# Two weight transfers for the first head of a fused attention and gated-MLP kernel, and a copy moved from GpSimd to ScalarE

## The chip, the cores and the metric

The kernel runs on one core of a Trainium2 chip. The metric is the device time of one execution in microseconds, as the median of three runs. Engines are named as in the profile: PE is TensorE (PEld its weight loads), DVE VectorE, ACT ScalarE, POOL GpSimd, SP SyncE, which issues most transfers.

## The reference

```python
x = A_x                                # [1, 2048, 640], bf16
xn = _layernorm(x)
q = (xn @ wq)                          # 32 heads of 192
scores = einsum("bhqd,bhkd->bhqk", q, k_cache) * (192 ** -0.5)   # 2048 keys
o = einsum("bhqk,bhkd->bhqd", softmax(scores), v_cache)
s = o.reshape(1, 2048, 32 * 192) @ wo  # back to 640
h = silu(xn @ w1) * (xn @ w3)          # 1536 hidden
g = silu(h @ w2)
return x + s * g
```

## The kernel before

The work goes head by head, in each head over four blocks of 512 queries (`qb`), in each block over eight pairs of key tiles (`p`). A projection fills two PSUM banks of 128 rows by 512 queries. A head has only 192 query columns, so the second bank's 64 free rows compute 64 columns of the MLP: even heads take a slice of `B_w1`, odd heads one of `B_w3`. The first bank (`t = 0`) is columns 0 to 127 of the head, the second (`t = 1`) has the MLP slice in rows 0 to 63 and columns 128 to 191 of the head in rows 64 to 127. After the projection the banks are cast to bf16 as `qA` (first bank) and `qF` (second); `qS` is `qA` with its two row halves swapped, `qD` the lower rows of `qF` moved up. The score matmuls contract over 64 rows each, so that two of them, one on the upper and one on the lower row half of the array, make a step; for that the keys lie as `KT` and, with halves exchanged, as `KM`.

The first head (h = 0) has routines of its own. Its weights come in pieces on SP's queue (`load_weights`, L99), issued between those of the keys. Its first block is projected at L380 with 128 contraction rows, in two halves of 256 queries. Its other blocks, and they alone besides a small part of the MLP, go through `by_halves` (L347): ten matmuls on the two row halves, then other work (`between`, mainly the values of an earlier step, L620), then ten more with the banks exchanged between the halves. The other heads are projected by `by_steps` (L362). From the third head on scores, values and projections are split into four 64x64 quarters (`quads`); the first two heads use 64x128.

The order of nearly all instructions is written out by hand (`pin` keeps them in program order on their engine). At the start, POOL builds `KM` from `KT` (L138, L135), shifts three columns of key maxima (`up`, `down`; L468, L471, L472), sets the column of ones in the values' tile (L141), and copies `qS` (L392) for the first block. DVE takes maxima of the keys (L411) and of the queries (L400), joins them (L477), and from them comes the bound `nbb` (L500, L502), without which ACT can't start the first exponential (L569). PE meanwhile runs `fill` matmuls (L224) that keep it busy, four of them in front of the first scores (L561). The order at the start is

```python
copy_high(L0); key_maxima(0, 1); up(m0); key_maxima(0, 2); copy_low(L0)
down(m0)
set_ones(L0)
key_maxima(0, 0)
project_chunk(0, 0, nc.scalar.copy)()
heads[0]["km"] = join_maxima(m0, sh)
```

where the call's result, called at once, takes the maxima of the queries. The functions that the change touches:

Of the kernel before, what the change touches and what calls it, by code (L numbers as in the profile page):

```python
# [12 lines left out]
BF16 = mybir.dt.bfloat16  # L13
# [3 lines left out]
P = 128  # L17
DH = 192
# [12 lines left out]
def _kernel_impl(ctx, tc, A_x, A_k_cache, A_v_cache, A_wq, A_wo, B_w1, B_w3, B_w2, out):  # L31
    nc = tc.nc
# [4 lines left out]
    DC = D // P  # L37
# [10 lines left out]
    PGW = P - DT  # L48
# [5 lines left out]
    ROWS = (slice(0, DT), slice(DT, P))  # L54
# [19 lines left out]
    xnT = const.tile([P, DC, SQ], BF16, name="xnT")  # L74

    pin = tc.keep_in_program_order
# [12 lines left out]
    def load_weights(h):  # L89
        wsel = B_w1 if h % 2 == 0 else B_w3  # L90
        m = h // 2
        parts = ((A_wq[:, h * DH:h * DH + P], 0, 0, P), (wsel[:, m * PGW:(m + 1) * PGW], 1, 0, PGW),
                 (A_wq[:, h * DH + P:(h + 1) * DH], 1, PGW, P))
        if h == 0:
            wq = lnx.tile([P, 2, DC, P], BF16, name="wq0")

            def piece(part):
                w, t, c0, c1 = part
                pin(nc.sync.dma_start(out=wq[:, t, :, c0:c1], in_=w.rearrange("(c p) d -> p c d", p=P)))  # L99
            return dict(wq=wq, pieces=[lambda part=part: piece(part) for part in parts])  # L100
        else:
            wq = wqp.tile([P, 2 * DC, P], BF16, tag="wq")
            for w, t, c0, c1 in parts:
                pin((nc.gpsimd if h <= 3 else nc.sync).dma_start(out=wq[ROWS[t], :, c0:c1], in_=w.rearrange("(s p) d -> p s d", p=DT)))
        return dict(wq=wq)
# [28 lines left out]
    def copy_low(L, keep=pin):  # L134
        keep(nc.gpsimd.tensor_copy(out=L["KM"][ROWS[0], :], in_=L["KT"][ROWS[1], 0, :]))  # L135
# [4 lines left out]
    def set_ones(L, keep=pin):  # L140
        keep(nc.gpsimd.memset(L["vt"][:, :, :, DH:DH + 1], 1.0))  # L141

    def move(out, in_):
        pin(nc.sync.dma_start(out=out, in_=in_))
# [28 lines left out]
    with ExitStack() as actx:  # L173
# [5 lines left out]
        lnx = lctx.enter_context(tc.tile_pool(name="lnx", bufs=1, side="right"))  # L179
# [7 lines left out]
        cols = lnx.tile([P, 32], BF16, name="cols")  # L187
        rows = lnx.tile([P, 32], BF16, name="rows")
        nc.vector.memset(cols[:, 0:1], 0.0)
        for k in range(5):  # L190
            w = 1 << k
# [146 lines left out]
        def by_halves(banks, w, qs, touch, between):  # L338
            def behind_of(op, dep):
                tc.add_manual_dep(op.ins, dep.ins.name, mybir.DependencyInfo(  # L340
                    mybir.DependencyClass.Sync, mybir.DependencyReason.DATA), reason="bank")

            for half in range(2):
                for c in range(DC):
                    for r in range(2):
                        t = r ^ half
                        mm = pin(nc.tensor.matmul(banks[t], lhsT=w(t, c)[ROWS[r], :], rhs=xnT[ROWS[r], c, qs],  # L347
                                                  start=(half == 0 and c == 0), stop=(half == 1 and c == DC - 1)))
                        if half == 1 and c == 0:
                            behind_of(mm, fence)  # L350
                if half == 0:
                    mark = fsb.tile([P, 1], F32, tag="mark", name="mark")
                    fence = pin(touch(out=mark[:], in_=eps_t[:]))
                    behind_of(fence, mm)
                    between()
# [9 lines left out]
        def project_chunk(h, qb, cast=nc.vector.tensor_copy, mid=(), quads=False, cast_low=None):  # L365
            hd = heads[h]
            wq = hd["L"]["wq"]
            qA, qF, qS, qD, st = hd["qA"], hd["qF"], hd["qS"], hd["qD"], hd["st"]
            qs = slice(qb * 512, (qb + 1) * 512)
            ps = ps_st.tile([P, 1024], F32, tag="st2", name="ps")  # L370
            halves = [ps[:, 0:512], ps[:, 512:1024]]
            if h == 0 and qb > 0:
                by_halves(halves, lambda t, c: wq[:, t, c, :], qs, nc.scalar.copy if qb == 1 else nc.vector.tensor_copy, steps((parts.pop(0)[1],), *mid))
            elif h == 0:
                acc["bp"] = ps_o.tile([P, 2, 512], F32, tag="ob0", name="bp")
                halves[1] = acc["bp"][:, 1, :]
                for u in (slice(0, 256), slice(256, 512)):
                    for t in range(2):
                        for c in range(DC):
                            pin(nc.tensor.matmul(halves[t][:, u], lhsT=wq[:, t, c, :], rhs=xnT[:, c, u],  # L380
                                                 start=(c == 0), stop=(c == DC - 1)))
            else:
                by_steps(halves, wq, qs, quads)
            for c, dst, src in ((cast_low or cast, qF, halves[1]), (cast, qA, halves[0]))[::1 if cast_low else -1]:
                pin(c(out=dst[:, qs], in_=src))  # L385
            if h > 1:
                move(qD[:, qs], qF[PGW:P, qs])
                for t in range(2):
                    move(qS[ROWS[t], qs], qA[ROWS[1 - t], qs])
                return None  # L390
            for t in range(2):
                pin(nc.gpsimd.tensor_copy(out=qS[ROWS[t], qs], in_=qA[ROWS[1 - t], qs]))  # L392

            first = h == 0 and qb == 0
            copy = nc.scalar.copy if first else nc.gpsimd.tensor_copy
            pin(copy(out=qD[:, qs], in_=qF[PGW:P, qs]))

            def maxima():
                for col, src, r0 in ((3, halves[0] if first else qA[:, qs], 0), (4, halves[1] if first else qF[:, qs], PGW)):
                    pin(nc.vector.tensor_reduce(out=st[r0:P, col, qb:qb + 1], in_=src[r0:P, :], axis=AX.X, op=ALU.max,  # L400
                                                apply_absolute_value=True))
            return maxima
# [6 lines left out]
        def key_maxima(h, j, k=0, n=1):  # L409
            c0, c1 = k * HALF // n, (k + 1) * HALF // n  # L410
            pin(nc.vector.tensor_reduce(out=heads[h]["st"][:, j, k:k + 1], in_=heads[h]["L"]["KT"][:, j, c0:c1], axis=AX.X,  # L411
                                        op=ALU.max, apply_absolute_value=True))
# [328 lines left out]
        parts = []  # L741
# [53 lines left out]
        up(m0)  # L795
        key_maxima(0, 2)
        copy_low(L0)
        down(m0)
        set_ones(L0)
        key_maxima(0, 0)  # L800
        project_chunk(0, 0, nc.scalar.copy)()
        heads[0]["km"] = join_maxima(m0, sh)
        loads[1] = load_weights(1)
        swap_rows(0)
# [27 lines left out]
        def steps(*fs):  # L832
            return lambda: [f(*a) for f, *a in fs]
# [77 lines left out]
        w1_sb = fw.tile([P, DC, FL - P], BF16, name="w1_sb")  # L911
        w3_sb = fw.tile([P, DC, FL - P], BF16, name="w3_sb")
# [18 lines left out]
        def ffn_hidden(qb, fl, ps, between=None):  # L931
            hT = get_hT(qb)
            qs = slice(qb * 512, (qb + 1) * 512)
            if between:
                by_halves((ps[:, 0:512], ps[:, 512:1024]), lambda t, c: (w1_sb, w3_sb)[t][:, c, (fl - 1) * P:fl * P], qs,
                          nc.vector.tensor_copy, between)
            else:
                for o, w_sb in ((0, w1_sb), (512, w3_sb)):
                    for c in range(DC):
                        pin(nc.tensor.matmul(ps[:, o:o + 512], lhsT=w_sb[:, c, (fl - 1) * P:fl * P], rhs=xnT[:, c, qs],  # L940
                                             start=(c == 0), stop=(c == DC - 1)))
            t = fsb.tile([P, 512], BF16, tag="t", name="t")
            pin(nc.scalar.activation(out=t[:], in_=ps[:, 0:512], func=ACT.Tanh, scale=0.5))
            u = fsb.tile([P, 512], BF16, tag="u", name="u")
            pin(nc.vector.tensor_copy(out=u[:], in_=ps[:, 512:1024]))
            a = fsb.tile([P, 512], BF16, tag="a", name="a")
            pin(nc.vector.scalar_tensor_tensor(out=a[:], in0=t[:], scalar=1.0, in1=ps[:, 0:512], op0=ALU.add, op1=ALU.mult))
            return lambda: pin(nc.vector.tensor_tensor(out=hT[:, FCP + fl - 1, :], in0=a[:], in1=u[:], op=ALU.mult))
# [249 lines left out]
    with ExitStack() as dctx:  # L1198
# [3 lines left out]
        with tc.issue_after(acc["store"].ins):  # L1202
            parts = [load_part(pools, 0, j) for j in range(3)]
# [30 lines left out]
        def st_bank():  # L1234
            return ps_st.tile([P, 1024], F32, tag="st2", name="ps_s")
# [4 lines left out]
        for qb in range(LB):  # L1240
            if qb == 0:
                banks = [st_bank(), st_bank(), ob_bank(0)]
            elif qb == 1:
                banks = [ob_bank(1), st_bank(), st_bank()]
            else:
                banks = [ob_bank(0), ob_bank(1), st_bank()]
# [162 lines left out]
```

## Time and profile before

| | |
|---|---|
| median of 3 runs | 1918.88 us (1918.73 to 1919.02) |
| profiled execution | 1919.53 us, span 1917.9 us |
| granted TensorE clock | 1.0 |
| PE busy | 1910.8 us |
| ACT, DVE, POOL busy | 1382.4, 1426.1, 99.7 us |

In a timeline each row has its start and its length in us, engine, line, operation, out<-in by the program's names, the tile of the array (rows*columns) for matmuls, operand shapes, the count that the row merges, and in brackets the engine's idle time before it with what ended it. Rows of one engine can overlap, since the end of a matmul is modelled and lies behind the start of the next.

### The profile page before, as it was taken

Reading aid. Unit: us, or ns where it says so; the run is one execution under the profiler, and the core shown is the slowest. Engines: PE = TensorE matmul, PEld = TensorE weight load, DVE = VectorE, ACT = ScalarE, POOL = GpSimd, SP = SyncE. Lnnn points to the kernel's source line nnn. Section 1 sums busy time; section 2 is a strip of 40 time slices with the busy share of each in tenths; the row PEclk is TensorE's granted clock in tenths of the full one; section 3 lists DMA queues with packets and bytes.
Section 4 is the critical chain, followed back from the end, with each engine's and each line's share of the span. In section 5 each row is a group of like instructions: output and inputs, shape, how many; then the busy total and the mean of one; then the engine's idle time right before and its main releaser. Section 6 shows DMA issues by size and latency. Waiting matters only on the chain.

```text
span 1917.9 us, 68799 instructions
## 1 busy us (share of the span) xinstructions
PE 1910.8 (100%) x30919; PEld 1112.4 (58%) x30919; DVE 1426.1 (74%) x2558; ACT 1382.4 (72%) x1521; POOL 99.7 (5%) x224
## 2 busy tenths in 40 slices
PE   9999999999999999999999999999999999999999
PEld 5665555555555555555555556666666666454456
DVE  8658888888888888888888888888888885521111
ACT  7778888888888888888888888888888887210000
POOL 3300000000000000000000000000000000000000
PEclk9999999999999999999999999999999999999999
DMA  7835655566655656566556565656565634937763
GB/s 169 151 74 101 134 111 123 114 121 115 127 119 113 129 108 128 107 128 117 130 106 132 101 132 100 138 96 141 104 125 112 131 60 125 273 82 150 165 151 76
DMA packets 649579, 235.86 MB, mean 123 GB/s; under 512 B 577072, under 2 KB 641168, under 8 KB 649280
## 3 DMA queue, kind: packets, MB, share of 16 engines
q1 hardware_dynamic: 640816, 210.98, 55.1%
q0 software_dynamic: 3776, 15.40, 2.8%
q10 hardware_dynamic: 4688, 5.05, 0.9%
q8 instruction: 242, 3.96, 0.9%
q14 instruction: 57, 0.47, 0.1%
HBM read 54.26 MB, written 31.98 MB: 45 GB/s over the span
## 4 chain that ended last, share of the span: by engine, by line
PE 99%; DMA 0%; POOL 0%; ACT 0%; issue 0%; SPq 0%; DVE 0%; POOLq 0%
PE st L561 34%; PE obank L640 31%; PE ps L362 14%; PE ps_s L1153 8%; PE obank L620 3%; PE ps_s L1109 3%; PE ps_f L1173 2%; PE ps_gu L940 1%; PE ps_f L1189 1%; PE ps L347 0%; DMA KT<-in_A_k_cache_dram 0%; PE ps_gu L347 0%; ACT xnT L290 0%; SPq L115 0%; PE pst L289 0%
## 5 line engine op out<-in xcount | busy, mean ns | idle before, releaser
L569 ACT ACTIVATE pT<-st,nb 128x1024 bf16<-128x1024 f32 x1016 | 1125.3, 1113 | 188.0 <-PE st L561 151.3
L640 PE MATMUL obank<-pT,vt 64*64 64x512 bf16 x11136 | 765.5, 376 | 0.0
L640 PEld LDWEIGHTS <-vt 64*64 64x64 bf16 x11136 | 360.7, 107 | 258.3
L561 PE MATMUL st<-qS,KM 64*64 64x512 bf16 (+1 forms) x1951 | 397.6, 376 | 0.5 <-POOL qS L392 0.5
L561 PE MATMUL st<-qD,KT 64*64 64x512 bf16 (+1 forms) x1951 | 397.6, 376 | 0.0
L561 PE MATMUL st<-qA,KT 64*64 64x512 bf16 (+1 forms) x1951 | 397.5, 376 | 0.0
L561 PE MATMUL st<-qA,KM 64*64 64x512 bf16 (+1 forms) x1951 | 391.4, 376 | 0.0
L561 PE MATMUL st<-qS,KT 64*64 64x512 bf16 (+1 forms) x1951 | 391.3, 376 | 0.1
L561 PE MATMUL st<-qF,KT 64*64 64x512 bf16 (+1 forms) x1951 | 391.3, 376 | 0.0
L561 PEld LDWEIGHTS <-KT 64*64 64x64 bf16 (+1 forms) x7808 | 249.4, 106 | 176.0 <-issue 0.6
L362 PE MATMUL ps<-xnT,wq 64*64 64x512 bf16 (+1 forms) x2390 | 289.5, 376 | 0.0
L362 PE MATMUL ps<-xnS,wq 64*64 64x512 bf16 (+1 forms) x2390 | 287.9, 376 | 0.0
L673 DVE TENSOR_TENSOR tree<-pT,pT 128x2048 bf16<-128x2048 bf16 x232 | 282.6, 1218 | 3.2 <-ACT pT L569 3.2
L665 DVE TENSOR_TENSOR ot<-oa,obank 128x512 bf16<-128x512 f32 x232 | 149.0, 683 | 108.6 <-ACT oa L664 108.1
L673 DVE TENSOR_TENSOR tree<-tree 128x2048 bf16<-128x2048 bf16 x232 | 221.2, 954 | 4.0
L362 PEld LDWEIGHTS <-wq 64*64 64x64 bf16 (+1 forms) x4780 | 151.4, 107 | 113.9
L561 PEld LDWEIGHTS <-KM 64*64 64x64 bf16 (+1 forms) x3904 | 132.4, 106 | 74.1 <-issue 1.4
L1153 PE MATMUL ps_s<-oT,wo_sb 128*128 128x512 bf16 x720 | 155.7, 379 | 0.0
L664 ACT COPY oa<-obank 128x512 f32<-128x512 f32 x232 | 123.6, 589 | 0.0
L1153 PEld LDWEIGHTS <-wo_sb 128*128 128x128 bf16 x720 | 70.4, 98 | 84.9 <-issue 0.2
L385 ACT CAST qF<-ps 128x512 bf16<-128x512 f32 x123 | 72.1, 586 | 60.1 <-PE ps L362 60.1
L1143 DVE SCALAR_TENSOR_TENSOR tmp<-ps_s,gT 128x512 f32<-128x512 f32 x15 | 10.3, 686 | 136.0 <-PE ps_s L1153 136.0
(160 smaller groups left out, 1440.6 us busy)
## 6 DMA issues: line engine op xcount, KB each, us to landing
o_scr<-ostage SPq DMA_DIRECT2D x64, 384.0 KB, 3.7
vt<-in_A_v_cache_dram SPq DMA_DIRECT2D x62, 384.0 KB, 5.0
qS<-qA SPq DMA_DIRECT2D x240, 64.0 KB, 2.0
qD<-qF SPq DMA_DIRECT2D x120, 64.0 KB, 2.1
KM<-KT SPq DMA_DIRECT2D x60, 128.0 KB, 5.1
wo_sb<-in_A_wo_dram POOLq DMA_DIRECT2D x1, 7680.0 KB, 31.8
wq<-in_A_wq_dram SPq DMA_DIRECT2D x29, 160.0 KB, 3.7
hT_scr<-hblk SPq DMA_DIRECT2D x16, 256.0 KB, 2.9
```

The lines of the kernel that those rows point to most:

```text
L362: pin(nc.tensor.matmul(halves[t][c, :], lhsT=w[ROWS[t], s, c], rhs=xs[ROWS[t], s // 2, qs], start=(s == 0), stop=(s == 2 * DC - 1)))
L385: pin(c(out=dst[:, qs], in_=src))
L561: pin(nc.tensor.matmul(st2[c, t * 512:(t + 1) * 512], lhsT=k[:, c], rhs=q[ROWS[t], qs], start=(s == 0), stop=(s == 2)))
L569: pin(nc.scalar.activation(out=pT2, in_=st2[:], func=ACT.Exp, scale=SCALE, bias=nb[:]))
L620: pin(nc.tensor.matmul(acc["o"][b][:, r, (j % 2) * 256:(j % 2) * 256 + DH + 1], lhsT=pT2[ROWS[r], t * 512 + j * P:t * 512 + (j + 1) * P], ...
L640: pin(nc.tensor.matmul(acc["o"][low][ROWS[c], r, :], lhsT=vt[ROWS[r], u, p, c0:c0 + DT], rhs=pT2[ROWS[r], u * 512:(u + 1) * 512], start=(p ...
L664: pin(nc.scalar.copy(out=oa[:], in_=bank[:, 0, :]))
L665: pin(nc.vector.tensor_tensor(out=ot[:, k * 512:(k + 1) * 512], in0=oa[:], in1=bank[:, 1, :], op=ALU.add))
L673: pin(nc.vector.tensor_tensor(out=out, in0=a, in1=b, op=ALU.add))
L1109: pin(nc.tensor.matmul(ps, lhsT=oT[:, k, :], rhs=wo_sb[:, k, c0:c1], start=(k == 0), stop=(k == OC - 1)))
L1153: pin(nc.tensor.matmul(ps_of[d], lhsT=wo_sb[:, k, d * P:(d + 1) * P], rhs=part(k // KQ)[:, k % KQ, :], start=(k == 0), stop=(k == OC - 1)))
L1173: pin(nc.tensor.matmul(ps[:, e * 512:(e + 1) * 512], lhsT=w2_sb[:, fc, d * P:(d + 1) * P], rhs=rhs[fc], start=(fc == 0), stop=(fc == FC - 1)))
```

## The change

The first head's weights lie in one tile of 256 columns per contraction chunk, first the head's 192 columns, then the 64 of `B_w1`, and are brought by two transfers (192 and 64 columns) in place of three (128, 64 and 64). The second bank's stationary operand is then in two parts, columns 192 to 255 for its upper rows and 128 to 191 for its lower ones, and each of its matmuls becomes two. In the first block the second `qS` copy moves from POOL to ACT, in front of that of `qD`; `down` and `set_ones` move behind POOL's first `qS` copy, and the maxima of the queries still follow those of the keys on DVE.

```diff
         if h == 0:
-            wq = lnx.tile([P, 2, DC, P], BF16, name="wq0")
-
-            def piece(part):
-                w, t, c0, c1 = part
-                pin(nc.sync.dma_start(out=wq[:, t, :, c0:c1], in_=w.rearrange("(c p) d -> p c d", p=P)))
-            return dict(wq=wq, pieces=[lambda part=part: piece(part) for part in parts])
+            wq = lnx.tile([P, DC, 2 * P], BF16, name="wq0")
+
+            def piece(w, c0, c1):
+                pin(nc.sync.dma_start(out=wq[:, :, c0:c1], in_=w.rearrange("(c p) d -> p c d", p=P)))
+
+            def cols(t, c):
+                if t == 0:
+                    return [(slice(0, P), wq[:, c, 0:P])]
+                return [(ROWS[0], wq[:, c, DH:2 * P]), (ROWS[1], wq[:, c, P:DH])]
+            return dict(wq=cols, pieces=[lambda: piece(A_wq[:, 0:DH], 0, DH), lambda: piece(B_w1[:, 0:PGW], DH, 2 * P)])
...
                         t = r ^ half
-                        mm = pin(nc.tensor.matmul(banks[t], lhsT=w(t, c)[ROWS[r], :], rhs=xnT[ROWS[r], c, qs],
-                                                  start=(half == 0 and c == 0), stop=(half == 1 and c == DC - 1)))
-                        if half == 1 and c == 0:
-                            behind_of(mm, fence)
+                        for o, wt in w(t, c):
+                            mm = pin(nc.tensor.matmul(banks[t][o, :], lhsT=wt[ROWS[r], :], rhs=xnT[ROWS[r], c, qs],
+                                                      start=(half == 0 and c == 0), stop=(half == 1 and c == DC - 1)))
+                            if half == 1 and c == 0:
+                                behind_of(mm, fence)
...
                         for c in range(DC):
-                            pin(nc.tensor.matmul(halves[t][:, u], lhsT=wq[:, t, c, :], rhs=xnT[:, c, u],
-                                                 start=(c == 0), stop=(c == DC - 1)))
+                            for o, wt in wq(t, c):
+                                pin(nc.tensor.matmul(halves[t][o, u], lhsT=wt, rhs=xnT[:, c, u],
+                                                     start=(c == 0), stop=(c == DC - 1)))
...
+            first = h == 0 and qb == 0
             for t in range(2):
-                pin(nc.gpsimd.tensor_copy(out=qS[ROWS[t], qs], in_=qA[ROWS[1 - t], qs]))
-
-            first = h == 0 and qb == 0
+                pin((nc.scalar.copy if first and t else nc.gpsimd.tensor_copy)(out=qS[ROWS[t], qs], in_=qA[ROWS[1 - t], qs]))
+
             copy = nc.scalar.copy if first else nc.gpsimd.tensor_copy
             pin(copy(out=qD[:, qs], in_=qF[PGW:P, qs]))
...
         copy_low(L0)
+        key_maxima(0, 0)
+        first_maxima = project_chunk(0, 0, nc.scalar.copy)
         down(m0)
         set_ones(L0)
-        key_maxima(0, 0)
-        project_chunk(0, 0, nc.scalar.copy)()
+        first_maxima()
         heads[0]["km"] = join_maxima(m0, sh)
```

The callers of `by_halves` pass `wq` as it is, or, in the MLP, a list with one entry, which leaves that part as it was.

More of the change, by code (lines that the diff above doesn't have):

```diff
@@ L372, in project_chunk @@
             if h == 0 and qb > 0:
-                by_halves(halves, lambda t, c: wq[:, t, c, :], qs, nc.scalar.copy if qb == 1 else nc.vector.tensor_copy, steps((parts.pop(0)[1],), *mid))
+                by_halves(halves, wq, qs, nc.scalar.copy if qb == 1 else nc.vector.tensor_copy, steps((parts.pop(0)[1],), *mid))
             elif h == 0:
@@ L934, in ffn_hidden @@
             if between:
-                by_halves((ps[:, 0:512], ps[:, 512:1024]), lambda t, c: (w1_sb, w3_sb)[t][:, c, (fl - 1) * P:fl * P], qs,
+                by_halves((ps[:, 0:512], ps[:, 512:1024]), lambda t, c: [(slice(0, P), (w1_sb, w3_sb)[t][:, c, (fl - 1) * P:fl * P])], qs,
                           nc.vector.tensor_copy, between)
```

## The prediction

> **What bounds the kernel now.** I read the engines' totals first, then the timeline of the first 45 us engine by engine, then the tensor engine's and its weight loads' timeline in two short windows where the matmuls change their tile shape.
>
> ```profile
> PE 1910.8 (100%) x30919; PEld 1112.4 (58%) x30919; DVE 1426.1 (74%) x2558; ACT 1382.4 (72%) x1521; POOL 99.7 (5%) x224
> ```
>
> TensorE (PE) is busy for 1910.8 of a span of 1917.9 us. So two things can move the time: idle time of PE before its steady stream starts, which is small, and anything that makes the stream itself longer, which counts in full. The change touches both. The start first, PE and then its suppliers:
>
> ```profile
> 9.50 0.71 PE L380 MATMUL ps<-xnT,wq 128*128 128x256 bf16 x5
> 10.04 0.71 PE L380 MATMUL bp<-xnT,wq 128*128 128x256 bf16 x5
> 10.65 0.70 PE L380 MATMUL ps<-xnT,wq 128*128 128x256 bf16 x5
> 11.20 0.71 PE L380 MATMUL bp<-xnT,wq 128*128 128x256 bf16 x5
> 11.74 1.03 PE L224 MATMUL fill<-ones_w,ones_bf 128*128 128x512 bf16 x4
> 13.31 0.37 PE L561 MATMUL st<-qS,KM 64*128 64x512 bf16 x1 [0.54 <-POOL qS L392]
> 13.31 0.39 PE L561 MATMUL st<-qA,KM 64*128 64x512 bf16 x1
> 13.52 0.37 PE L561 MATMUL st<-qA,KT 64*128 64x512 bf16 x1
> 13.97 0.37 PE L561 MATMUL st<-qS,KT 64*128 64x512 bf16 x1
> 13.98 0.39 PE L561 MATMUL st<-qD,KT 64*128 64x512 bf16 x1
> 14.19 0.37 PE L561 MATMUL st<-qF,KT 64*128 64x512 bf16 x1
> 14.49 0.20 PE L500 MATMUL bp<-prb,ones_bf 128*128 128x1 bf16 x2
> ```
>
> ```profile
> 11.40 0.59 ACT L385 CAST qA<-ps 128x512 bf16<-128x512 f32 x1 [0.79 <-PE ps L380]
> 11.94 0.59 ACT L385 CAST qF<-bp 128x512 bf16<-128x512 f32 x1
> 12.56 0.62 ACT L396 COPY qD<-qF 64x512 bf16<-64x512 bf16 x1
> 14.92 2.12 ACT L569 ACTIVATE pT<-st,nbb 128x1024 bf16<-128x1024 f32 x2 [1.75 <-DVE nbb L502]
> ```
>
> ```profile
> 10.95 1.04 POOL L135 COPY KM<-KT 64x1024 bf16<-64x1024 bf16 x1
> 12.05 0.18 POOL L471 COPY sh<-st 64x1 f32<-64x1 f32 x1
> ...
> 12.64 1.27 POOL L392 COPY qS<-qA 64x512 bf16<-64x512 bf16 x2
> ```
>
> GpSimd (POOL) is the late one: its two swapped copies end at 13.27 and 13.91. PE waits 0.54 us for the first, and its fourth score matmul starts at 13.97, right behind the second. The small matmul of L500, from which the first exponentials hang (through nbb), stands behind these scores in PE's order.
>
> **The change, part by part: the start.** On POOL the two `down` copies and the memset go behind the first qS copy, so that copy needs only KM (done 11.99) and qA (done 11.99): it could start at 12.05 in place of 12.64. The second copy goes to ScalarE (ACT) behind the casts of qA and qF, in front of qD's copy; half of the 1.27 us on POOL and the 0.62 us of qD's copy on ACT are the same price, so qD comes 0.62 us later than its 13.18. On POOL the two copies of `down` (0.18 each, the first at 12.05 now) then end about 0.4 us behind the first qS copy; the vector engine (DVE) joins the maxima only here:
>
> ```profile
> 12.88 0.69 DVE L400 TENSOR_REDUCE st<-bp 64x1 f32<-64x512 f32 x1
> 13.61 0.33 DVE L477 TENSOR_TENSOR km<-st,sh 128x2 f32<-128x2 f32 x1
> 13.97 0.16 DVE L492 SCALAR_TENSOR_TENSOR prb<-km,st 128x2 bf16<-128x2 f32 x1
> ```
>
> so that wait is covered by DVE's own maximum until 13.57 and costs nothing while POOL is done by then. What is queued behind on POOL are the transfers of L104 and L407, which start about half a microsecond earlier. Behind ACT's extra copy stands the pT of 14.92, which waits for nbb anyway.
>
> The transfers:
>
> ```profile
> 5.09 0.58 SPq L99 DMA_DIRECT2D wq<-in_A_wq_dram  x1
> 5.71 0.53 SPq L99 DMA_DIRECT2D wq<-in_B_w_dram  x1
> 6.29 0.53 SPq L99 DMA_DIRECT2D wq<-in_A_wq_dram  x1
> ```
>
> ```profile
> wq<-in_A_wq_dram SPq DMA_DIRECT2D x1, 160.0 KB, 3.4
> wq<-in_A_wq_dram SPq DMA_DIRECT2D x1, 80.0 KB, 3.3
> ```
>
> One issue of 0.53 us goes, and KT's third plane and all that follows on SP's queue start that much sooner. Its readers (POOL's L135 at 10.95 among them) run directly behind their own engines' earlier work, so this is worth nothing. The first transfer grows from 160 to 240 KB. It landed at 8.5 (5.09 + 3.4). If its time goes by rows it still does; if by bytes, half as much again, at 10.2, 0.7 us behind the 9.50 at which PE uses it. Its 640 rows are as many as before and the last piece landed at 9.6 with all 320 KB on the way, so I take no delay and keep +0.7 for the range.
>
> **The change on PE.** The second output bank now has its two 64-column parts apart in memory, so each of its matmuls becomes two with 64 stationary columns. In the first block that is 10 of 20, in the shape 128*64, which the trace doesn't show. One bound: each two run side by side, as the four 64*64 below do; the other: one after the other, 10 x 0.11 = +1.1 us (five took 0.54, 11.20 to 11.74). I take side by side. But the shape alternates, and a change of shape has a price in this trace:
>
> ```profile
> 127.85 0.59 PE L362 MATMUL ps<-xnS,wq 64*128 64x512 bf16 x2
> 128.06 0.38 PE L362 MATMUL ps<-xnT,wq 64*128 64x512 bf16 x1
> 128.37 0.40 PE L561 MATMUL st<-qS,KM 64*64 64x512 bf16 x1
> ...
> 128.61 0.38 PE L561 MATMUL st<-qA,KT 64*64 64x512 bf16 x1
> ```
>
> ```profile
> 127.42 0.53 PEld L362 LDWEIGHTS <-wq 64*128 64x128 bf16 x6
> 128.37 0.11 PEld L561 LDWEIGHTS <-KM 64*64 64x64 bf16 x4 [0.42 <-issue]
> ```
>
> ```profile
> 1580.34 0.38 PE L362 MATMUL ps<-xnT,wl 64*64 64x512 bf16 x1
> 1580.65 0.39 PE L561 MATMUL st<-qS,KM 64*128 64x512 bf16 x1
> ```
>
> From start to start 0.31 us pass where the shape changes, in either direction (128.06 to 128.37, 1580.34 to 1580.65), in place of the 0.21 to 0.22 of an unchanged shape, and the step after it is up to 0.025 longer (128.37 to 128.61). The weight loads, which otherwise run ahead, sit idle for 0.42 us and start with the first matmul of the new shape. So a change costs 0.095 to 0.12 us, and everything of the new shape waits until the old has streamed through.
>
> In the first block: four changes. The third group of five starts at 9.50 + 2 x 0.54 + 2 x 0.1 = 10.78 (10.65 before), so qA's cast runs from 11.53 to 12.12 and POOL's copy from 12.17 to 12.80. The fourth group starts at 11.42 and ends at 12.13, so qF's cast runs from 12.18, the second qS copy from 12.71 to 13.33 (0.53 from cast to next, as at 11.40 and 11.94) and qD's to 13.9. The fill matmuls come 0.32 later (12.06 for 11.74), so scores start at about 13.02 (0.31 behind the last of four 0.215 apart), the fourth at 13.4 and, with the last two, those of qD and qF at 13.94; L500 follows 0.30 behind the last score (14.19 to 14.49), at 14.25 in place of 14.49. Worth -0.2 us in all; without any price for changes it would be limited by qD and by prb (ready 14.13) to about 14.2, -0.3. With the pairs one after the other it would be +0.6.
>
> Then the part that weighs most. Blocks 1 to 3 of the first head are projected at L347 by halves:
>
> ```profile
> 36.63 1.24 PE L347 MATMUL ps<-xnT,wq 64*128 64x512 bf16 x10
> 37.71 0.50 PE L620 MATMUL obank<-vt,pT 64*128 64x193 bf16 x8
> ```
>
> Ten matmuls take 1.08 us (36.63 to 37.71), in five pairs of 0.216: one on the upper 64 rows and one on the lower, side by side. After the change one of each pair is a 64*128 and the other two 64*64. If the shapes cannot be in the array together, each pair becomes a 64*128, a change, two 64*64 abreast, a change: 2 x 0.31 us and up to 2 x 0.025 more, so 0.62 to 0.67 in place of 0.216. The values between the halves are 64*128, so each half still has ten changes. That is 5 pairs x 2 halves x 3 blocks = 30 pairs, 0.405 to 0.455 each: 12.2 to 13.6 us, and I take 12.5, nearer to the low end, since the longer step is shown for one direction only. Nothing covers it, PE being the bound there.
>
> What the rows leave open is whether the wait holds for two shapes on different row halves, since at both places the next matmul uses rows that the last one still occupied. [...]
>
> Sum against the profiled execution: 1919.53 + 12.5 - 0.2 = 1931.8 us. That execution lies 0.65 above the median of the runs, 1918.88, so for the median 1931.2.
>
> **The rivals.** First, not slower: the row halves are independent whatever the shapes, so that the 64*128 on one half and the two 64*64 on the other run abreast as the pairs at 36.63 do. Then the 30 pairs keep their 0.216 us and only the start is left: 1918.88 - 0.3 = 1918.6, within the bound. For it speaks that the two halves start together and finish apart today (the one at 13.52 ran on its half while the other half's stood until 13.97); against it that both halves' weight loads stood idle at 128.37. It decides from the first pair: start to start near zero, or 0.31. [...]
>
> Second: the price of the change is due, but the halves overlap: 60 changes x 0.095 to 0.12 = 5.7 to 7.2, and with 6.1 and the start 1924.8. Nothing speaks for it but that the price and the lost overlap are separate things.
>
> Third: the two 64-column matmuls don't run abreast either: 30 x 0.215 = 6.5 more and +0.8 at the start, 1938.4. Against it: four 64*64 start between 128.37 and 128.61 in one step of 0.24.
>
> **How the numbers follow.** Forecast (both price and lost overlap) 0.77, the independent halves 0.13, price alone 0.05, one after the other 0.03; 0.02 is left for a gain that I cannot see, since the start holds less than 1 us of waits. Within 0.2% is within 3.8 us, about what a measurement of this kernel can tell from no change: 0.13. Slower 0.85, faster 0.02. The forecast's own range is 1930.8 to 1933.8 (12.2 to 13.6, the start from -0.3 to +0.6 + 0.7); to hold 8 in 10 I reach down to the price alone with its low end (5.7 - 0.3), 1924.3 to 1933.8, and leave out the independent halves and the 1938.
>
> **What would show it.** Right: in the matmuls that L347 issues today, 64*128 and 64*64 alternating with 0.31 us or a little more from start to start, each half 3.1 to 3.3 us rather than 1.08, weight loads idle before each change; L500 at about 14.25; qS's first copy on POOL at about 12.2, the second on ACT at about 12.7. Wrong: halves of about 1.1 us, or PE waiting for wq at 9.50, or an L500 later than 14.49.

## The result, and the profile after

The changed kernel takes 1931.71 us (median of 6 runs, 1931.22 to 1935.48) against 1918.94 (6 runs, 1918.73 to 1919.05): ratio 1.007, 95% interval 1.0059 to 1.008. It is 12.8 us slower; the forecast was 1931.2. The run of 1935.48 had a mean granted clock of 0.997, the other five 1.0. The profiled execution has 1931.71 us and a span of 1930.1, 12.2 more than before.

The engines' totals of the changed kernel:

```profile
PE 1924.3 (100%) x30959; PEld 1227.7 (64%) x30959; DVE 1427.4 (74%) x2558; ACT 1381.8 (72%) x1522; POOL 98.9 (5%) x223
```

PE has 40 matmuls more and is busy 13.5 us longer; DVE, ACT and POOL stand as before. Where it lies is seen in PE's timeline (start, length) at the first projection by halves. The line that was L347 is now L352, the values' L620 is L626:

```profile
23.15 3.31 PE L352 MATMUL ps<-xnT,wq 64*128 64x512 bf16 x15 [0.17 <-ACT xnT L294]
26.40 0.51 PE L626 MATMUL obank<-vt,pT 64*128 64x193 bf16 x8
26.84 3.33 PE L352 MATMUL ps<-xnT,wq 64*64 64x512 bf16 x15
29.79 0.39 PE L567 MATMUL st<-qS,KM 64*128 64x512 bf16 x1
```

A row merges one line's matmuls under the shape of the first. The first half takes 3.25 us (23.15 to 26.40) where 1.08 stood. The second takes 2.95 until the scores begin; its last wide (64*128) matmul, whose weights load at 29.78, still runs beside the first score matmul, so that the scores on the lower rows come one step later. The weight loads of the same stretch show why:

```profile
23.45 0.11 PEld L352 LDWEIGHTS <-wq 64*64 64x64 bf16 x2 [0.75 <-issue]
23.79 0.09 PEld L352 LDWEIGHTS <-wq 64*128 64x128 bf16 x1 [0.23 <-issue]
24.11 0.11 PEld L352 LDWEIGHTS <-wq 64*64 64x64 bf16 x2 [0.23 <-issue]
24.44 0.09 PEld L352 LDWEIGHTS <-wq 64*128 64x128 bf16 x1 [0.23 <-issue]
```

The shapes alternate every 0.32 to 0.34 us, and before each the weight loads stand idle for 0.23 us or more. The first matmul, on the upper rows, started at 23.15; the narrow ones on the lower rows, which were free, were not loaded until 23.45. So one step for both banks is 0.65 us (23.79 to 24.44) in place of 0.216.

At the start, PE, then ACT and POOL:

```profile
1.88 5.71 PE L228 MATMUL fill<-ones_w,ones_bf 128*128 128x512 bf16 x13 [1.88 <-DVE cols L193]
...
9.76 0.71 PE L386 MATMUL ps<-xnT,wq 128*128 128x256 bf16 x5
10.39 0.74 PE L386 MATMUL bp<-xnT,wq 128*64 128x256 bf16 x10
11.06 0.72 PE L386 MATMUL ps<-xnT,wq 128*128 128x256 bf16 x5
11.71 0.74 PE L386 MATMUL bp<-xnT,wq 128*64 128x256 bf16 x10
12.38 1.04 PE L228 MATMUL fill<-ones_w,ones_bf 128*128 128x512 bf16 x4
13.35 0.39 PE L567 MATMUL st<-qS,KM 64*128 64x512 bf16 x1
...
14.41 0.37 PE L567 MATMUL st<-qD,KT 64*128 64x512 bf16 x1 [0.27 <-ACT qD L402]
...
14.74 0.20 PE L506 MATMUL bp<-prb,ones_bf 128*128 128x1 bf16 x2
```

```profile
11.82 0.59 ACT L391 CAST qA<-ps 128x512 bf16<-128x512 f32 x1 [0.97 <-PE ps L386]
12.49 0.58 ACT L391 CAST qF<-bp 128x512 bf16<-128x512 f32 x1
13.10 0.62 ACT L399 COPY qS<-qA 64x512 bf16<-64x512 bf16 x1
13.74 0.62 ACT L402 COPY qD<-qF 64x512 bf16<-64x512 bf16 x1
```

```profile
12.47 0.61 POOL L399 COPY qS<-qA 64x512 bf16<-64x512 bf16 x1 [1.20 <-ACT qA L391]
13.13 0.18 POOL L477 COPY sh<-st 64x1 f32<-64x1 f32 x1
```

POOL is no longer late; PE now waits 0.27 us for qD on ACT. The small matmul of the bound (now L506) follows the first projection matmul by 4.98 us (9.76 to 14.74), as in the profiled execution before (9.50 to 14.49: 4.99). In this execution PE reached that projection 0.26 us later, behind first fill matmuls that took 5.71 us. Before they took less:

```profile
1.88 5.09 PE L224 MATMUL fill<-ones_w,ones_bf 128*128 128x512 bf16 x13 [1.88 <-DVE cols L189]
```

The code ahead of that point is the same, so distances from the first projection matmul are compared below, not times from the start.

### The profile page after: what moved, and what is told of

Read it like the earlier page. It is cut to its first block, busy times and chain, and to the rows that moved or that the text cites. A ratio compares the mean times of both kernels' runs of the same rounds, so it can differ in the third digit from the quotient of the medians.

```text
span 1930.1 us, 68875 instructions
## 1 busy us (share of the span) xinstructions
PE 1924.3 (100%) x30959; PEld 1227.7 (64%) x30959; DVE 1427.4 (74%) x2558; ACT 1381.8 (72%) x1522; POOL 98.9 (5%) x223
## 4 chain that ended last, share of the span: by engine, by line
PE 99%; ACT 0%; DVE 0%; issue 0%
PE st L567 34%; PE obank L646 31%; PE ps L367 14%; PE ps_s L1160 8%; PE obank L626 3%; PE ps_s L1116 3%; PE ps_f L1180 2%; PE ps_gu L947 1%; PE ps L352 1%; PE ps_f L1196 1%; PE fill L228 0%; PE ps_gu L352 0%; PE pst L293 0%; PE bp L386 0%; ACT xnT L294 0%; PE ps L386 0%
## 5 line engine op out<-in xcount | busy, mean ns | idle before, releaser
L646 PE MATMUL obank<-pT,vt 64*64 64x512 bf16 x11136 | 781.5, 376 | 0.0
L646 PEld LDWEIGHTS <-vt 64*64 64x64 bf16 x11136 | 406.7, 107 | 211.8
L567 PE MATMUL st<-qD,KT 64*64 64x512 bf16 (+1 forms) x1951 | 413.5, 376 | 0.3 <-ACT qD L402 0.3
L567 PE MATMUL st<-qS,KM 64*64 64x512 bf16 (+1 forms) x1951 | 413.7, 376 | 0.0
L567 PE MATMUL st<-qA,KT 64*64 64x512 bf16 (+1 forms) x1951 | 413.6, 376 | 0.0
L567 PEld LDWEIGHTS <-KT 64*64 64x64 bf16 (+1 forms) x7808 | 281.7, 106 | 144.7 <-DMA vt<-in_A_v_cache_dram 0.5
L367 PEld LDWEIGHTS <-wq 64*64 64x64 bf16 (+1 forms) x4780 | 171.5, 107 | 93.9
L567 PEld LDWEIGHTS <-KM 64*64 64x64 bf16 (+1 forms) x3904 | 147.9, 106 | 59.4 <-issue 0.8
```

What stands on the lines that cost most here:

```text
L367: pin(nc.tensor.matmul(halves[t][c, :], lhsT=w[ROWS[t], s, c], rhs=xs[ROWS[t], s // 2, qs], start=(s == 0), stop=(s == 2 * DC - 1)))
L567: pin(nc.tensor.matmul(st2[c, t * 512:(t + 1) * 512], lhsT=k[:, c], rhs=q[ROWS[t], qs], start=(s == 0), stop=(s == 2)))
L646: pin(nc.tensor.matmul(acc["o"][low][ROWS[c], r, :], lhsT=vt[ROWS[r], u, p, c0:c0 + DT], rhs=pT2[ROWS[r], u * 512:(u + 1) * 512], start=(p ...
```

## The experiments

The theory: the two shapes cannot be in the array together, so in blocks 1 to 3 each pair is taken apart and each change of shape costs 0.1 us (0.095 to 0.12 in the rows of the kernel before); the start and the transfers are worth next to nothing. The rivals: the split itself (more and narrower matmuls) costs; the start or the transfers cost; or it is all price of changes.

**The order at the start alone.** The kernel before, with

```diff
-            for t in range(2):
-                pin(nc.gpsimd.tensor_copy(out=qS[ROWS[t], qs], in_=qA[ROWS[1 - t], qs]))
+            for t in range(2):
+                pin((nc.scalar.copy if first and t else nc.gpsimd.tensor_copy)(out=qS[ROWS[t], qs], in_=qA[ROWS[1 - t], qs]))
...
+        key_maxima(0, 0)
+        first_maxima = project_chunk(0, 0, nc.scalar.copy)
         down(m0)
         set_ones(L0)
-        key_maxima(0, 0)
-        project_chunk(0, 0, nc.scalar.copy)()
+        first_maxima()
```

> The weights stay as before (three transfers, whole second bank); only the order at the start is changed (second qS copy on ACT, down and set_ones behind POOL's first qS copy, first maxima behind the keys'). Theory (the loss is the alternation of 64*128 and 64*64 in by_halves): the time is that of before or up to 0.3 us less, 1918.6 to 1919.0. In the changed kernel PE waited 0.27 us for qD on ACT, so most of the gain on POOL is given back there: I expect the L500 matmul between 14.2 and 14.5 and not at 14.14. Rival (the start is part of the loss, through ACT's extra copy): 1919.2 to 1919.6.

1919.26 us against 1919.03 on the same chip, ratio 1.0001 (0.9992 to 1.001). PE's timeline:

```profile
1.88 4.31 PE L224 MATMUL fill<-ones_w,ones_bf 128*128 128x512 bf16 x13 [1.88 <-DVE cols L189]
...
9.37 0.71 PE L380 MATMUL ps<-xnT,wq 128*128 128x256 bf16 x5
...
13.73 0.37 PE L561 MATMUL st<-qD,KT 64*128 64x512 bf16 x1 [0.27 <-ACT qD L396]
...
14.05 0.20 PE L500 MATMUL bp<-prb,ones_bf 128*128 128x1 bf16 x2
```

The bound comes 4.68 us after the first projection matmul, against 4.99 in the one profiled execution of the kernel before, with the same 0.27 us of waiting for qD. In the time no gain shows. The start is not where the loss is.

**The weights alone.** The changed kernel with that diff undone.

> Only the weights' layout, the two transfers and the split matmuls; the order at the start as before. Theory: three blocks at 4.26 us each (the lag behind the kernel before grows by that much in each of the three blocks in the trace of the changed kernel) and up to 0.3 us at the start: 1931.7 to 1932.1. Rival (part of the loss is the order at the start): below 1931.4.

1931.57 us, ratio 1.0071 (1.0056 to 1.0086): all of the loss, just under the range expected. With the old order at the start the bound comes sooner than in the changed kernel, 4.75 us after the first projection matmul against 4.98:

```profile
9.51 0.71 PE L386 MATMUL ps<-xnT,wq 128*128 128x256 bf16 x5
...
14.26 0.20 PE L506 MATMUL bp<-prb,ones_bf 128*128 128x1 bf16 x2
```

**All in quarters.** The changed kernel, where the first bank is split as well:

```diff
-                by_halves(halves, wq, qs, nc.scalar.copy if qb == 1 else nc.vector.tensor_copy, steps((parts.pop(0)[1],), *mid))
+                by_halves(halves, lambda t, c: wq(t, c) if t else [(ROWS[0], wq(0, c)[0][1][:, 0:DT]), (ROWS[1], wq(0, c)[0][1][:, DT:P])],
+                          qs, nc.scalar.copy if qb == 1 else nc.vector.tensor_copy, steps((parts.pop(0)[1],), *mid))
```

> As the changed kernel, but in by_halves of the first head the first bank's matmuls are split into two 64-column parts too, so all are 64*64: 20 matmuls and weight loads in a half in place of 15, and four changes of shape in a block (before and behind each half) in place of 20. Theory (mixing of shapes): each half about 1.1 to 1.2 us plus its two changes of 0.1, so some 0.4 us a block over the kernel before and 0.1 to 0.3 at the start: 1920.2 to 1920.6. Rival (the split itself costs: more matmuls, more and narrower weight loads): at least as slow as the changed kernel, 1931.7 or more.

1920.13 us, ratio 1.0005 (0.9996 to 1.0015), just under the range expected: 1.1 us over the kernel before. PE's timeline:

```profile
22.78 1.27 PE L352 MATMUL ps<-xnT,wq 64*64 64x512 bf16 x20 [0.16 <-ACT xnT L294]
23.98 0.51 PE L626 MATMUL obank<-vt,pT 64*128 64x193 bf16 x8
24.42 1.27 PE L352 MATMUL ps<-xnT,wq 64*64 64x512 bf16 x20
25.63 0.39 PE L567 MATMUL st<-qS,KM 64*128 64x512 bf16 x1
```

Twenty narrow matmuls of one shape take 1.2 us (22.78 to 23.98), fifteen mixed ones took 3.25. More and narrower matmuls of one shape cost at most a few tenths of a microsecond a block; as the cause of the loss that rival falls.

**Grouped by shape.** The changed kernel with the two loops of a half exchanged, so that in the first half the five wide ones come before the ten narrow ones, and in the second the ten before the five:

```diff
-                for c in range(DC):
-                    for r in range(2):
+                for r in range(2):
+                    for c in range(DC):
```

> As the changed kernel, but in each half first the five matmuls of one bank, then the ten narrow ones of the other (or the reverse): four changes of shape in a block in place of 20, and no two shapes next to each other, so that no pair can run side by side. Theory (price of a change about 0.1 us, and lost overlap 0.215 us for each of the ten pairs of a block): 2.15 + 4 x 0.11 = 2.6 us a block, 1926.6 to 1927.0 in all. Rival (all of the 4.26 us of a block is the price of its 20 changes, 0.21 each): 4 x 0.21 = 0.85 us a block, 1921.5. Rival (the number of narrow matmuls): as the changed kernel, 1931.7.

1926.59 us, ratio 1.0039 (1.0024 to 1.0054). Its weight loads in the first half:

```profile
22.77 0.74 PEld L352 LDWEIGHTS <-wq 64*128 64x128 bf16 x4 [0.45 <-issue]
23.93 0.79 PEld L352 LDWEIGHTS <-wq 64*64 64x64 bf16 x10 [0.42 <-issue]
25.13 0.28 PEld L626 LDWEIGHTS <-pT 64*128 64x128 bf16 x8 [0.41 <-issue]
```

Only two halts at a change of shape are left in the half (23.93 and 25.13), which takes 2.36 us (22.77 to 25.13). The time is 7.56 us over the kernel before (1919.03), so 2.5 a block with four changes and no wide matmul beside its two narrow ones; the changed kernel's 12.8 are 4.26 a block with twenty changes and again none. If a change costs the same in both, sixteen changes make 1.74 us, 0.11 each, within the 0.095 to 0.12 read from the rows of the kernel before, and what is left, 2.1 us for the ten such sets of a block, is the lost overlap: a step of 0.21 for each. All of it as price of changes is out, which would have been 1921.5.

**Whole columns for blocks 1 to 3.** The changed kernel, with columns 128 to 191 of the head loaded once more by a third, late transfer, to a place right behind the MLP's columns; the first block keeps its split matmuls.

```diff
-            wq = lnx.tile([P, DC, 2 * P], BF16, name="wq0")
+            wq = lnx.tile([P, DC, 2 * P + PGW], BF16, name="wq0")
...
+            def whole(t, c):
+                return [(slice(0, P), wq[:, c, DH:2 * P + PGW] if t else wq[:, c, 0:P])]
+            return dict(wq=cols, whole=whole, low=lambda: piece(A_wq[:, P:DH], 2 * P, 2 * P + PGW), ...
...
         load_x(nc.sync, 12, 16)
+        first_w["low"]()
...
-                by_halves(halves, wq, qs, ...
+                by_halves(halves, hd["L"]["whole"], qs, ...
```

> The changed kernel, with the head's columns 128 to 191 loaded once more by a late third transfer right behind the MLP's columns, so that the second bank's 128 columns lie together for blocks 1 to 3: these use whole 64*128 matmuls as before, the first block keeps its split ones. Theory (mixing shapes in by_halves is all of the loss): each half 1.08 us again, 1918.8 to 1919.4 in all, with the two early transfers and the order at the start kept. Rival (part of the loss comes from elsewhere, the first block's split or the transfers): 1919.6 or more. The late transfer has about ten microseconds until its first use.

> As the run before it, but with the order at the start as in the kernel before (both qS copies on POOL, down in front of them). Theory: no alternation, so 1918.9 to 1919.5; between this and the run before it at most 0.3 us. Rival (the order at the start is worth more once the split of the first block delays PE): 1919.6 or more.

Both missed: 1921.71 us (1920.48 to 1924.12) and 1922.70 (1919.03 to 1923.39), against 1919.07. PE's timeline and the DMA issues of the first:

```profile
23.19 0.37 PE L356 MATMUL ps<-xnT,wq 64*128 64x512 bf16 x1 [0.17 <-ACT xnT L298]
25.81 1.25 PE L356 MATMUL ps<-xnT,wq 64*128 64x512 bf16 x9 [2.25 <-DMA wq<-in_A_wq_dram]
```

```profile
x_all<-in_A_x_dram SPq DMA_DIRECT2D x2, 640.0 KB, 7.6
...
wq<-in_A_wq_dram SPq DMA_DIRECT2D x1, 80.0 KB, 13.0
```

The 80 KB, issued behind the last two pieces of x on the same queue, took 13.0 us. My ten microseconds of cover were too few. In the second kernel the wait was 3.00 us:

```profile
9.43 0.71 PE L390 MATMUL ps<-xnT,wq 128*128 128x256 bf16 x5
...
14.02 0.20 PE L510 MATMUL bp<-prb,ones_bf 128*128 128x1 bf16 x2
...
25.82 2.31 PE L356 MATMUL ps<-xnT,wq 64*128 64x512 bf16 x9 [3.00 <-DMA wq<-in_A_wq_dram]
```

The nine matmuls behind the wait took 2.31 us, those of the first kernel 1.25. The table by stretches (busy times of PE, PEld, DVE, ACT and POOL, granted clock, DMA share, GB/s) shows a lower clock there:

```profile
25.00:30.00 5.00, 4.18 (x31) 2.82 (x33) 0.80 (x2) 0.70 (x4) 0.00 (x0) 0.66 0.01 4
```

The granted clock was 0.66 in the five microseconds in which that wait ended (25.82); in the same stretch of the first kernel, behind 2.25 us, it was 1.00. Of the second kernel's eleven executions the eight with a mean granted clock of 0.999 took 1922.48 us or more, the three with 1.0 at most 1920.60.

**The third transfer ahead of x's last pieces.**

```diff
+        first_w["low"]()
         load_x(nc.sync, 8, 12)
         load_x(nc.sync, 12, 16)
-        first_w["low"]()
```

> As the run with the joined low columns and the changed kernel's start, but the third transfer is issued ahead of the last two pieces of x instead of behind them. In the earlier run PE waited 2.25 us for that transfer, which took 13.0 us from issue to landing. Theory (that wait was all that kept it from the time of before): no wait at the first by_halves matmul, each half 1.08 us, 1918.9 to 1919.6. Rival (joined columns cost something beside the wait, or the wait moves to x's last pieces): 1920 or more.

1918.69 us (1918.51 to 1918.92) against 1918.99 on the same chip, ratio 0.9998 (0.9989 to 1.0007), a little below what was expected.

```profile
23.10 1.26 PE L356 MATMUL ps<-xnT,wq 64*128 64x512 bf16 x10 [0.16 <-ACT xnT L298]
24.18 0.51 PE L630 MATMUL obank<-vt,pT 64*128 64x193 bf16 x8
```

```profile
wq<-in_A_wq_dram SPq DMA_DIRECT2D x1, 80.0 KB, 5.3
```

The transfer takes 5.3 us, the wait is gone, and the half is 1.08 us again (23.10 to 24.18). With the two early transfers, the split first block and the order at the start all kept, the 12.8 us are gone, to within 0.1% of the time: mixing shapes in blocks 1 to 3 was the whole of the loss that can be measured.

**Only the deferral at the start.** The kernel before, with `down`, `set_ones` and the maxima moved as in the first experiment, both copies left on POOL; run twice. And the last kernel with the same start.

> The kernel before with one part of the change: down and set_ones behind POOL's qS copies and the first maxima behind the keys', both copies still on POOL, qD's copy on ACT not delayed. In the run with all of the start's edits the L500 matmul came 4.68 us after PE's first L380 matmul (9.37 to 14.05), 4.99 in the kernel before (9.50 to 14.49), with 0.27 us of waiting for qD. Theory (the second copy on ACT only moves the wait from POOL to qD): the same gain of 0.2 to 0.3 us without it, L500 4.7 us after the first L380; now the joined maxima, whose inputs POOL delivers last, are what it waits for. Rival (the copy on ACT is what gains): L500 at 4.9 to 5.0. In the time of the whole at most 0.3 us either way, 1918.6 to 1919.2.

> The run with only down, set_ones and the maxima deferred, once more, since its 0.2 us below the kernel before lay within the spread of the runs. Theory (half a microsecond less until L500 is kept to the end, PE having no slack behind it): 0.2 to 0.5 us below the runs of the kernel before on the same chip. Rival (the start is given back by what varies from run to run): no difference.

> The same with both qS copies on POOL and only down and set_ones behind them, the order that brought the L500 matmul 4.52 us after the first L380 (4.99 in the kernel before, 4.68 with the copy on ACT). The first block still has its split matmuls and four changes of shape, about 0.4 us. Theory: L500's successor at about 4.8 us after the first L380, as its prb is delayed by the split: 1918.7 to 1919.3. Rival (with PE delayed by the split POOL's two copies in a row are late again): 5.0 or more, 1919.3 to 1919.7.

1918.84 us against 1919.07 (0.9998, 0.9989 to 1.0007), 1918.69 against 1918.99 (0.9999, 0.999 to 1.0008), and for the combination 1918.53 against 1918.99 (0.9998, 0.9989 to 1.0007). PE in the first of these:

```profile
9.29 0.71 PE L380 MATMUL ps<-xnT,wq 128*128 128x256 bf16 x5
...
13.81 0.19 PE L500 MATMUL bp<-prb,ones_bf 128*128 128x1 bf16 x2
```

4.52 us between the two, and 4.56 (9.48 to 14.04) when it was run again: better than with the copy on ACT (4.68). In the combination they stand 5.03 apart, the rival's figure, since POOL's maxima came late there (PE, then DVE):

```profile
9.40 0.71 PE L390 MATMUL ps<-xnT,wq 128*128 128x256 bf16 x5
...
14.43 0.19 PE L510 MATMUL bp<-prb,ones_bf 128*128 128x1 bf16 x2
```

```profile
14.03 0.16 DVE L487 TENSOR_TENSOR km<-st,sh 128x2 f32<-128x2 f32 x1 [0.52 <-POOL sh L482]
```

That does not show the rival right: in this execution POOL's second key copy ended 3.11 us after the first projection matmul, 2.55 and 2.64 in the two others, and POOL's `qS` copies come right behind it. And yet the median of the combination is the lowest of all. A start that moves by a few tenths can be read in the trace and not told in the time: all these intervals hold 1. These are the best versions seen, by 0.2 to 0.5 us of the medians, and none is shown to beat the kernel before.

## Why the prediction was right

- *The bound.* PE's stream has no slack: the lag behind the kernel before grew in the three blocks, by 4.24, 4.26 and 4.27 us (12.77 in all), worked out from the starts of equal matmuls in the two traces, and was kept to the end. Forecast 12.5, with 12.2 to 13.6 as bounds. That is 2.08 for each half; the second halves lost that, the first ones 2.17. There the step after a change was longer in both directions (0.32 and 0.33 from start to start), not in one only, which is the 0.3 that was missing.
- *The open point.* No row of the trace before shows whether the halt holds for two shapes on different row halves; that it does was my estimate, from the weight loads that stood idle for 0.42 us before 128.37. It is settled by the matmul at 23.15 and the weight loads at 23.45: the loads for the free rows waited 0.30 us, though the row halves differed. The first rival, and with it 1918.6, is out.
- *Price alone and pairs one after the other* are both out: the grouped kernel separates price and overlap, and its ten narrow matmuls take 1.2 us with the change behind them (23.93 to 25.13), five steps of 0.216 and one change.
- *The start.* Forecast -0.2; measured from the first projection matmul, 0.0 (4.98 and 4.99). Counted from the start of the span, the bound's matmul came at 14.74, past the 14.49 that the forecast had named as a sign of being wrong; 0.26 of that is the later projection. The step that failed is ACT's: I put its copies 0.53 us apart like the casts, from 12.71, and so qD at 13.9; they are 0.61 to 0.64 apart (12.49, 13.10, 13.74), like the cast and the copy behind it in the kernel before (11.94 and 12.56). So qD came 0.2 us later than forecast and took the gain. The four groups of the first block took 2.62 us (9.76 to 12.38) in place of 2.24 (9.50 to 11.74): 0.38 more, 0.32 forecast. The narrow pairs ran abreast, ten matmuls in 0.74.
- *What the copy on ACT is worth.* The 4.99 of the kernel before is one execution. In the old order the bound follows the end of POOL's second key copy, which varies: 2.49 us after the first projection matmul there, 2.25 and 2.09 in the two kernels that have the split weights with the old order, whose bounds stand at 4.75 and 4.59. With the copy on ACT and the split weights it stands at 4.98 in all five traces that have both (the changed kernel's, the quarters', the grouped one's and two of those with whole columns), right behind the scores that wait for qD. So in these traces the moved copy makes the start of the changed kernel no earlier, and rather 0.2 to 0.4 us later; no time shows it.
- *The transfers.* No wait for wq, as forecast: PE's projection stood right behind its fills. The 240 KB took 3.4 us from issue to landing, as the 160 KB had before.
- *The sum.* The two misses, 0.3 in the blocks and 0.2 at the start, have the same sign and make the 0.5 between 1931.2 and 1931.7. The span grew by 12.2 us, less than the 13.0 by which PE's last matmul moved (12.77 and 0.25 at the start). The 0.8 lie in the last transfer of the output: its 32 KB took 2.3 us from issue to landing in the profiled execution before and 1.5 in the one after.

## What to carry to other kernels

Before a matmul is split to suit a layout, look at the shapes of its neighbours in the engine's order. Here, with moving operands of 512 columns, two shapes that alternate cost each step its overlap (0.21 us) and 0.11 us for every change, while twenty narrow matmuls in one shape took 1.2 us where ten wide ones take 1.08. If the layout has to stay, make all of a stretch one shape, or have the operand a second time in the order in which it is used, and send that transfer ahead of the bulk ones (5.3 us here, 13.0 behind them). A few tenths at the start are judged from one fixed instruction to another, not from the total, and from more than one execution.

## What the runs showed of the hardware that was not expected

- The same thirteen fill matmuls took 4.31, 5.09 and 5.71 us in three executions with the same code ahead of them; the first projection matmul came at 9.37, 9.50 and 9.76. From start to start they stand 0.43 us apart at first and 0.22 later; that change came after eleven matmuls in the second, not within the thirteen in the third, and in the first after about seven, worked out from its length, while the granted clock of the profile read 1.00 from 2 to 8 us in the second and the third and 1.0 over the whole execution in all three.
- After PE had stood for 3.00 us the granted clock was 0.66 in the stretch from 25 to 30 us, and the nine matmuls behind the wait took 2.31 us, so that it cost more than its length; after 2.25 us the clock was still 1.00 and the same nine took 1.25. These are one execution each.
- A transfer of 80 KB in rows of 128 bytes took 13.0 us behind two of 640 KB on the same queue, and 5.3 in front of them.
